# Key sums by TensorE for eight head pairs, denominators by one VectorE pass, silus of tile 0 in pairs, and a new planned order

## The chip, the cores and the metric

The kernel runs on one core of one Trainium2 chip. The metric is the device time of one execution in microseconds (us). The core has a matrix engine (TensorE, PE in the profile; PEld is its weight load), a vector engine (VectorE, DVE), a scalar engine (ScalarE, ACT), GpSimd (POOL) and a sync engine (SyncE, SP) that issues DMAs. Each engine runs its own instructions in the order in which the program gives them; engines wait for one another through semaphores.

## The reference

A linear attention with exponential features feeds a two-layer perceptron. There are 8 batches, 8 heads, 576 positions, head size 64, 128 features, and 4608 tokens of width 512 with an inner width of 2048.

```python
def phi(x):                       # x is q or k, scaled
    proj = einsum('bhsd,md->bhsm', x, omega)
    h = proj - sum(x * x, -1, keepdims=True) / 2
    return exp(h - max(h, -1, keepdims=True)) / sqrt(m)
kv  = einsum('bhsm,bhsd->bhmd', phi(k), v)
z   = sum(phi(k), axis=2)                         # the key sums
num = einsum('bhsm,bhmd->bhsd', phi(q), kv)
den = einsum('bhsm,bhm->bhs', phi(q), z)[..., None] + 1e-06
x   = (num / den), heads side by side             # 4608 x 512
h   = x @ w_in
out = (h * sigmoid(h)) @ w_out
```

## The kernel before

**Attention.** The work goes in 32 rounds n, each one pair of heads of one batch. A round has 9 chunks (NC) of 128 rows: four of the first head, one mixed chunk (MID) whose upper and lower 64 rows belong to different heads, four of the second. Per round and for k and q: `project` (L262) and `project_mid` (L269) on TensorE, row maxima `top` (L276, L278), row sums of squares `square_sum` (L254) and the exponent's shift `shift` (L282, L283) on VectorE, and the exponential on ScalarE, straight out of PSUM for n < 8 (DIRECT, `expo` L298), and after a VectorE pass (`lower`, L303 and L306) for the others. Then the key sums: `sums` adds the chunks on GpSimd with five instructions (L318, L320, L323), `zsum` multiplies with ones on TensorE (L327), so that the sum stands in every partition, and `zcopy` takes it to SBUF with four copies on ScalarE (L335, L336). The denominators: `products` makes e times z on VectorE with three instructions (L362), `denom` reduces them and takes the reciprocal (L369, L370). `normal` scales the query features on GpSimd (L375), `turn` transposes them (L381), `kv` (L343) and `numer` (L399) make the numerators, and `x_high` and `x_low` (L413, L418) split the result into two parts of x.

**Perceptron.** It goes in 9 tiles t of 512 tokens and 16 steps f per tile. Tile t < 8 takes positions 0 to 511 of batch t, so tile 0 needs rounds 0 to 3; tile 8 takes what is left over. `stage1` (L495) makes 12 matmuls into one bank of PSUM ring "h", which has two banks, `silu` (L500, L501) two activations, `g_low` (L505) one VectorE pass that frees the bank, and `stage2` (L513) 12 matmuls, two steps later (LAG). Each of the 32 weight blocks is prepared on the chip during tile 0: one pass on ScalarE (L442), three on VectorE (L456, L458, L462), two on GpSimd (L476, L480). The exponential and the silu lie in different activation tables of ScalarE, so a change between them costs a table load, which the trace puts on the line of the next activation.

**Order.** The program's order is made by a planner, `Plan.run`. Every piece of work is a unit with an engine, a duration, a key (its due time), units it comes after, and ring slots it takes and frees. The planner plays the engines forward with these durations and gives out, at each moment, the ready unit with the smallest key. The result is only an order of instructions on each engine; what waits for what on the chip is set by data and buffers. `at`, `clock`, START_MLP, PRO and STEP make the keys. The rounds n < 4 (LEAD) are given keys 11 us apart.

Of the kernel before, what the change touches and what calls it, by code (L numbers as in the profile page):

```python
# [56 lines left out]
CALM = 0.5  # L57


def clock(step):  # L60
    return START_MLP + SLOW * min(step, 16) + STEP * max(step - 16, 0)


class Plan:
# [6 lines left out]
    def add(self, name, eng, dur, key, fn, after=(), order=(), alloc=(), free=(), banks=0, table=None, lat=0.0):  # L71
# [9 lines left out]
    def run(self):  # L81
        end, first = {}, {}
        slots = {r: [] for r in RINGS}
# [27 lines left out]
        def bank_pools(u):  # L111
# [3 lines left out]
            if u["key"] < START_MLP - 1:  # L115
                pools.append("h")
# [14 lines left out]
        while any(ready.values()):  # L131
            best = None
            for e, us in ready.items():
                pick, least = None, None
                for u in us:
# [21 lines left out]
                    t = max(t, free_at[e])  # L157
# [30 lines left out]
            order.append(u)  # L188
            for c in children.get(n, ()):
# [8 lines left out]
def attention_mlp(ctx: ExitStack, tc: tile.TileContext, qT, kT, qn, kn, v, om_in, w_in, w_out, out):  # L198
# [19 lines left out]
    prod = const.tile([P, NC, M + 1], F32, tag="prod", name="prod")  # L218
    nc.gpsimd.memset(prod, GUARD)
# [328 lines left out]
    for n in range(NWIN):  # L548
        calm = n < LEAD
        for i, who in enumerate("kq"):  # L550
# [25 lines left out]
            for j in range(3):  # L576
                add(("top", n, who, j), "DVE", 0.3 if j == 2 else 0.7,
                    at(n, 3 * i + 1 + 0.1 * j, o + 1.2 + (4.5 if j == 2 else 0.1 * j)),
                    lambda n=n, who=who, j=j: top(n, who, j), after=[md if j == 2 else pj])
            if calm:  # L580
                add(("nb", n, who, 0), "DVE", 0.45, at(n, 3 * i + 1.5, 0), lambda n=n, who=who: shift(n, who, every),
                    after=[("top", n, who, j) for j in range(3)] + [("ssum",) + w], free=[("ss",) + w])
            else:
                add(("nb", n, who, 0), "DVE", 0.5, at(n, 0, o + 1.4), lambda n=n, who=who: shift(n, who, sides),
                    after=[("top", n, who, j) for j in range(2)] + [("ssum",) + w])
                add(("nb", n, who, 2), "DVE", 0.4, at(n, 0, o + 5.8), lambda n=n, who=who: shift(n, who, middle),
                    after=[("top", n, who, 2), ("ssum",) + w], free=[("ss",) + w])
# [15 lines left out]
        add(("v", n), "SP", 0.42, at(n, -8, 26 - 32), lambda n=n: load_v(n), order=[("v", n - 1)] if n else [],  # L603
            alloc=[("v", ("v", n))], lat=1.2)
# [16 lines left out]
        add(("ktt", n), "PE", 0.12, at(n, 6.7, 36.5), lambda ps, n=n: kv_turn(n, ps), after=[("kt", n)], banks=1,  # L621
# [3 lines left out]
        add(("prod", n), "DVE", 1.7, at(n, 8, 34.2), lambda n=n: products(n),  # L625
            after=e["q"] + [("zc", n)], order=[("den", n - 1)] if n else [], free=[("zb", n)])
        add(("den", n), "DVE", 1.6, at(n, 8.1, 34.4), lambda n=n: denom(n), after=[("prod", n)],
            alloc=[("den", ("den", n)), ("rd", ("rd", n))])
# [14 lines left out]
        dur = 1.4  # L643
        if follow:
# [3 lines left out]
            dur = 2.6  # L648
# [7 lines left out]
        add(("rest", n), "SP", 0.8, at(n, 20, 64), lambda n=n: keep_rest(n), after=[("xl", n, 0), ("xl", n, 1)], lat=0.2,  # L656
            free=[("x", t, k)])

    def weight(i, key, src, last, more=()):
        add(("wl",) + i, "SP", 0.42, key - 12, lambda: load_weight(src, i), order=[("wl",) + last] if last else [],  # L660
# [3 lines left out]
        for s in range(3):  # L664
            add(("wd",) + i + (s,), "DVE", (0.5, 0.78, 0.75)[s], key - 2 + 0.1 * s, lambda s=s: word(i, s),
# [3 lines left out]
                free=([("wraw",) + i] if s == 2 else [("wre",) + i] if s == 1 else []))  # L669
        add(("wh",) + i, "POOL", 0.9, key - 1, lambda: weight_high(i), after=[("wd",) + i + (2,)], alloc=list(more))  # L670
        add(("wlo",) + i, "POOL", 1.05, key, lambda: weight_low(i), after=[("wh",) + i], free=[("w32",) + i])

    last = None
    for f in range(NF):
# [6 lines left out]
        add(("keep", f), "SP", 0.42, clock(f + LAG) + 4, lambda f=f: keep_weight(f), after=[("wlo", "out", f)], lat=2.1,  # L681
# [3 lines left out]
    for k in range(NK):  # L685
        add(("restin", k), "SP", 0.8, clock(NF * B - 4), lambda k=k: load_rest(k),
            after=[("rest", n) for n in range(k, NWIN, NPAIR)], alloc=[(f"x{k}", ("x", B, k))], lat=2.2)
    done = None
    for i, (t, f) in enumerate(steps):
        key = clock(i)  # L690
        late = i >= total - LAG
        add(("get", t, f), "SP", 0.42, clock(i + LAG - AHEAD_OUT), lambda t=t, f=f: get_weight(t, f),
# [9 lines left out]
        add(("silu", t, f), "ACT", 1.22, key + STEP * 0.55, lambda t=t, f=f: silu(t, f), after=[("s1", t, f, NK - 1)],  # L702
# [3 lines left out]
        for j in range(4):  # L706
# [68 lines left out]
```

## Time and profile before

| | us |
|---|---|
| median of 3 runs | 1090.24 (1089.62 to 1092.56) |
| the profiled execution, its own time | 1089.61 |
| its span, first to last instruction | 1087.5 |
| PE busy | 1040.2 (96%) |
| DVE busy | 572.1 (53%) |
| ACT busy | 574.3 (53%) |
| POOL busy | 254.6 (23%) |

The busy times are averages over stages that differ. The page's forty slices show DVE at nine tenths up to about 190 us and at five tenths from there, PE at five to eight tenths at first and at nine from about 80 us on, and TensorE's granted clock below full speed up to about 100 us. So the span is read in stretches. A "chain" below is the chain of work that ended last, followed back from the last instruction.

### The profile page before, as it was taken

What the parts mean: (1) busy time and instruction counts of PE and PEld (TensorE: products, weight loads), DVE (VectorE), ACT (ScalarE), POOL (GpSimd) and SP (SyncE); (2) the same over time, 40 slices, a digit from 0 to 9 for tenths busy, and PEclk for the clock granted to TensorE, in tenths of its full rate; (3) what the DMA queues carried; (4) which work ended last, traced back from release to release, by engine and by line L of the source; (5) the groups of instructions that cost most, each with busy time, mean ns of one, the idle gap of its engine ahead of it and who ended that gap; (6) DMA issues with size and microseconds to landing.
All of it is one profiled execution on the core that took longest, in us unless ns stands there. A gap on an engine that the chain in (4) does not pass through costs nothing.

```text
span 1087.5 us, 16156 instructions
## 1 busy us (share of the span) xinstructions
PE 1040.2 (96%) x5900; PEld 825.2 (76%) x5900; DVE 572.1 (53%) x1109; ACT 574.3 (53%) x1077; POOL 254.6 (23%) x327
## 2 busy tenths in 40 slices
PE   5678998999999999999999999999999999999997
PEld 4456776677877778777877777777788778888886
DVE  6999988745555555545555555555555421111111
ACT  5677776565556555655556555655554543112111
POOL 3766655411222222121122211222222200000000
PEclk7868999999999999999999999999999999999999
DMA  7766777754435443544345444534442226333323
GB/s 274 248 220 228 271 249 243 238 176 141 141 123 176 128 126 118 175 141 130 123 133 172 126 136 141 180 122 137 130 157 89 65 83 213 97 97 126 107 97 97
DMA packets 66526, 167.84 MB, mean 154 GB/s; under 512 B 15632, under 2 KB 15760, under 8 KB 66448
## 3 DMA queue, kind: packets, MB, share of 16 engines
q1 hardware_dynamic: 65984, 166.23, 47.6%
q8 instruction: 47, 0.77, 0.3%
q10 hardware_dynamic: 464, 0.59, 0.2%
q14 instruction: 31, 0.25, 0.1%
HBM read 146.87 MB, written 19.92 MB: 153 GB/s over the span
## 4 chain that ended last, share of the span: by engine, by line
PE 80%; DVE 9%; ACT 6%; DMA 2%; issue 2%; POOL 0%; ACTq 0%; SPq 0%; DVEq 0%; POOLq 0%
PE ps_h L495 33%; PE ps_acc L513 32%; PE ps_att L262 5%; PE ps_att L343 3%; PE ps_att L381 2%; PE ps_att L399 2%; DVE w L458 1%; PE ps_att L327 1%; ACT L500 1%; DVE w L462 1%; PE ps_att L269 1%; DVE w L456 1%; DMA out<-ot 1%; DVE prod L362 1%; DMA wo_d<-wp 1%
## 5 line engine op out<-in xcount | busy, mean ns | idle before, releaser
L513 PE MATMUL ps_acc<-wo,gh 128*128 128x512 f32 x1152 | 369.0, 401 | 0.0
L500 ACT ACTIVATE gh<-ps_h 128x512 fp32r<-128x512 f32 x144 | 86.2, 599 | 308.4 <-PE ps_h L495 307.8
L505 DVE TENSOR_TENSOR gl<-ps_h,gh 128x512 fp32r<-128x512 f32 x144 | 97.9, 680 | 283.7 <-ACT ps_h L501 283.6
L513 PEld LDWEIGHTS ps_acc<-wo,gh 128*128 128x128 f32 x1152 | 206.2, 188 | 43.3
L495 PE MATMUL ps_h<-xh,wh 128*128 128x512 f32 x576 | 237.7, 413 | 0.3 <-ACT xh L413 0.3
L495 PE MATMUL ps_h<-xl,wh 128*128 128x512 f32 x576 | 225.5, 392 | 2.9 <-DVE xl L418 2.9
L495 PE MATMUL ps_h<-xh,wl 128*128 128x512 f32 x576 | 226.1, 393 | 0.0
L513 PE MATMUL ps_acc<-wo,gl 128*128 128x512 f32 x576 | 225.6, 392 | 0.0
L375 POOL TENSOR_TENSOR hq<-hq,rd 128x384 f32<-128x384 f32 x96 | 78.5, 846 | 380.0 <-DVE rd L370 375.3
L495 PEld LDWEIGHTS ps_h<-xh,wh 128*128 128x128 f32 x576 | 108.6, 189 | 24.8 <-ACT xh L413 0.5
L495 PEld LDWEIGHTS ps_h<-xl,wh 128*128 128x128 f32 x576 | 108.9, 189 | 24.1 <-DVE xl L418 3.3
L495 PEld LDWEIGHTS ps_h<-xh,wl 128*128 128x128 f32 x576 | 108.6, 188 | 24.5
L513 PEld LDWEIGHTS ps_acc<-wo,gl 128*128 128x128 f32 x576 | 108.1, 188 | 23.4
L318 POOL TENSOR_TENSOR t<-hk 128x256 f32<-128x256 f32 x64 | 48.8, 781 | 202.7 <-ACT hk L312 190.5
L312 ACT ACT_TABLE_LOAD x48 | 61.6, 1283 | 55.7 <-DVE hq L303 49.6
L501 ACT ACTIVATE ps_h<-ps_h 128x512 f32<-128x512 f32 x144 | 85.4, 593 | 0.0
L500 ACT ACT_TABLE_LOAD x56 | 71.8, 1283 | 22.7 <-PE ps_h L495 22.0
L278 DVE TENSOR_REDUCE mxq<-ps_att 128x4 f32<-128x512 f32 x57 | 36.9, 685 | 85.4 <-PE ps_att L262 85.4
L362 DVE TENSOR_TENSOR prod<-hq,zb 128x512 f32<-128x512 f32 (+1 forms) x96 | 53.0, 607 | 41.1 <-ACT zb L336 40.8
L250 ACT ACTIVATE nat<-nat 128x576 f32<-128x576 f32 x64 | 44.3, 700 | 23.4 <-DMA nat<-kn 18.6
L381 PE MATMUL ps_att<-ident,hq 128*128 128x128 f32 x261 | 41.0, 284 | 6.0 <-DVE hk L306 1.6
L278 DVE TENSOR_REDUCE mxk<-ps_att 128x4 f32<-128x512 f32 x55 | 35.5, 686 | 16.8 <-PE ps_att L262 16.8
(120 smaller groups left out, 1199.1 us busy)
## 6 DMA issues: line engine op xcount, KB each, us to landing
wo<-wo_d SPq DMA_DIRECT2D x144, 512.0 KB, 3.4
rawk<-kT SPq DMA_DIRECT2D x32, 352.0 KB, 3.0
rawq<-qT SPq DMA_DIRECT2D x32, 352.0 KB, 4.0
v<-v SPq DMA_DIRECT2D x32, 320.0 KB, 3.0
nat<-kn SPq DMA_DIRECT2D x32, 288.0 KB, 3.1
nat<-qn SPq DMA_DIRECT2D x32, 288.0 KB, 3.3
wraw<-w_in SPq DMA_DIRECT2D x16, 512.0 KB, 4.1
wraw<-w_out SPq DMA_DIRECT2D x16, 512.0 KB, 4.8
```

The lines of the kernel that those rows point to most:

```text
L262: nc.tensor.matmul(ps[:, i * M : (i + 1) * M], raw[r, o : o + P], oms[r], start=True, stop=True)
L278: nc.vector.tensor_reduce(m[:, 5 * j : 5 * j + 4], ps.rearrange("p (c m) -> p c m", m=M), AX.X, ALU.max)
L312: nc.scalar.activation(h, h, AF.Exp)
L318: nc.gpsimd.tensor_tensor(t[:, j], e[:, 5 * j : 5 * j + 2], e[:, 5 * j + 2 : 5 * j + 4], ALU.add)
L362: nc.vector.tensor_tensor(prod[:, c, :M], e[:, c], zb[:, j].unsqueeze(1).broadcast_to([P, hi - lo, M]), ALU.mult)
L375: nc.gpsimd.tensor_tensor(e[:, c], e[:, c], rd[:, c].unsqueeze(2).broadcast_to([P, 3, M]), ALU.mult)
L381: nc.tensor.transpose(ps[:, i * P : (i + 1) * P], T["h", n, "q"][:, 3 * g + i], ident)
L495: nc.tensor.matmul(ph, w[:, k, :], x, start=k == 0 and n == 0, stop=k == NK - 1 and n == 2)
L500: nc.scalar.activation(gh, ph, AF.Silu)
L501: nc.scalar.activation(ph, ph, AF.Silu)
L505: nc.vector.tensor_tensor(gl, T["ph", t, f], T["gh", t, f].bitcast(F32), ALU.subtract)
L513: nc.tensor.matmul(T["po", t][j], g[:, js], w, start=f == 0 and n == 0, stop=f == NF - 1 and n == 2)
```

## The change

For n < 8, `sums`, `zsum` and `zcopy` go. `zsum_direct` makes the key sums with ten matmuls straight from the nine chunks: the mixed chunk against one of two masks (`sides_of`), the others against ones. `denom_direct` multiplies chunk by chunk from PSUM and accumulates in the same instruction: ten instructions of 128 columns, two of them on 64 partitions. For n >= 8 `sums`, `zsum` and `zcopy` stay, and the denominators are nine such instructions from SBUF. In tile 0, the silu of an even step waits for the matmuls of the step after it. The planner gets other durations, a rule that units with `port` and units on POOL exclude one another, a rule that PE's units take 1.7 times as long after a pause, and shifts the keys of early units by random numbers of nine fixed seeds.

```diff
+SHIFTS = (1000, 1089, 1092, 1094, 1104, 1123, 1144, 1173, 1236,)
+def shift_keys(units):
+    early = [u for u in units if u["key"] < 235]
+    for seed in SHIFTS:
+        r = random.Random(seed)
+        part, wide = ((0.02, 6.0), (0.06, 3.0), (0.2, 1.5))[seed % 3]
+        for u, d in [(u, r.gauss(0, wide)) for u in early if r.random() < part]:
+            u["key"] += d
...
-            banks=banks, table=table, lat=lat,
+            banks=banks, table=table, lat=lat, port=port or eng == "POOL",
...
-                    t = max(t, free_at[e])
+                    t = max(t, free_at[e], port if u["port"] else 0.0)
...
+            if e == "PE":
+                if t - free_at[e] > 2.5:
+                    warm = t + 4.0
+                if t < warm:
+                    dur *= 1.7
             free_at[e] = t + dur
+            if u["port"]:
+                port = t + dur
...
-            if u["key"] < START_MLP - 1:
+            if u["key"] < START_MLP - 1 and ("s1", 0, 0, 0) not in end:
                 pools.append("h")
...
-    prod = const.tile([P, NC, M + 1], F32, tag="prod", name="prod")
-    nc.gpsimd.memset(prod, GUARD)
+    sides_of = const.tile([P, 2, P], F32, tag="sides", name="sides")
+    nc.gpsimd.memset(sides_of, 0.0)
+    for j in range(2):
+        nc.gpsimd.memset(sides_of[j * D : (j + 1) * D, j], 1.0)
+    prod = const.tile([P, NC, M], F32, tag="prod", name="prod")
...
+    def zsum_direct(n, ps):
+        e = T["h", n, "k"]
+        for j in range(2):
+            nc.tensor.matmul(ps[:, j * M : (j + 1) * M], sides_of[:, j], e[:, MID], start=True, stop=False)
+            for i in range(4):
+                nc.tensor.matmul(ps[:, j * M : (j + 1) * M], ones, e[:, 5 * j + i], start=False, stop=i == 3)
+        T["z", n] = ps
+
+    def denom_direct(n):
+        e, z = T["h", n, "q"], T.pop(("z", n))
+        den = new("den", [P, NC])
+        for c in range(NC):
+            for j in range(2) if c == MID else [int(c > MID)]:
+                r = slice(j * D, (j + 1) * D) if c == MID else slice(0, P)
+                nc.vector.tensor_tensor_reduce(
+                    out=prod[r, c], in0=e[r, c], in1=z[r, j * M : (j + 1) * M], scale=1.0, scalar=GUARD, op0=ALU.mult,
+                    op1=ALU.add, accum_out=den[r, c : c + 1],
+                )
+        T["rd", n] = rd = new("rd", [P, NC])
+        nc.vector.reciprocal(rd, den)
...
-    def products(n):
+    def denom(n):
         e, zb = T["h", n, "q"], T.pop(("zb", n))
-        for j, (lo, hi) in enumerate(((0, 4), (4, 5), (5, 9))):
-            c = slice(lo, hi)
-            nc.vector.tensor_tensor(
-                prod[:, c, :M], e[:, c], zb[:, j].unsqueeze(1).broadcast_to([P, hi - lo, M]), ALU.mult
+        den = new("den", [P, NC])
+        for c in range(NC):
+            j = (c >= MID) + (c > MID)
+            nc.vector.tensor_tensor_reduce(
+                out=prod[:, c], in0=e[:, c], in1=zb[:, j], scale=1.0, scalar=GUARD, op0=ALU.mult, op1=ALU.add,
+                accum_out=den[:, c : c + 1],
             )
-    def denom(n):
-        den = new("den", [P, NC])
-        nc.vector.tensor_reduce(den, prod, AX.X, ALU.add)
         nc.vector.reciprocal(rd, den)
...
+        if n < DIRECT:
+            add(zn, "PE", 2.3, at(n, 6.2, 31), lambda ps, n=n: zsum_direct(n, ps), after=e["k"], order=[("mid", n, "q")],
+                banks=1, free=[("h", n, "k")])
+        else:
+            add(("sums", n), "POOL", 3.3, at(n, 6, 25), lambda n=n: sums(n), after=e["k"], order=[("sums", n - 1)] if n > DIRECT else [],
...
+        if n < DIRECT:
+            add(("den", n), "DVE", 2.8, at(n, 8, 34.2), lambda n=n: denom_direct(n), after=e["q"] + [zn],
+                order=[("den", n - 1)] if n else [], alloc=[("den", ("den", n)), ("rd", ("rd", n))], free=[bk(zn)])
+        else:
+            add(("den", n), "DVE", 2.4, at(n, 8, 34.2), lambda n=n: denom(n), after=e["q"] + [("zc", n)], port=True,
...
-        add(("silu", t, f), "ACT", 1.22, key + STEP * 0.55, lambda t=t, f=f: silu(t, f), after=[("s1", t, f, NK - 1)],
+        pair = t == 0 and f % 2 == 0
+        add(("silu", t, f), "ACT", 1.12, key + STEP * (1.55 if pair else 0.55), lambda t=t, f=f: silu(t, f),
+            after=[("s1", t, f + pair, NK - 1)],
             alloc=[("gh", ("gh", t, f))], table="silu")
...
+    shift_keys(plan.units.values())
```

The units with `port` are the weight passes on VectorE, `shift`, and `denom` for n >= 8; the three products and the pass `denom_direct` are not among them.

## Rows read from the trace of the kernel before

**Rows 1.** Stretches: us, then busy us of PE, PEld, DVE, ACT, POOL; clock, DMA.

```profile
0.00:30.00 30.00, 18.86 (x144) 14.77 (x144) 21.36 (x39) 18.18 (x55) 11.97 (x20) 0.77 0.73 261
30.00:90.00 60.00, 38.48 (x268) 26.26 (x263) 58.72 (x98) 41.24 (x124) 39.88 (x45) 0.74 0.75 245
90.00:210.00 120.00, 111.65 (x638) 85.65 (x639) 110.52 (x177) 85.42 (x170) 75.20 (x78) 0.99 0.74 248
210.00:1000.00 790.00, 789.28 (x4499) 630.99 (x4498) 370.16 (x780) 411.52 (x695) 127.52 (x187) 1.00 0.43 134
```

**Rows 2.** The chain that ended last: start us, us, engine, tile, line, instructions.

```profile
16.68 0.43 PE ps_h L269 x2
...
38.76 0.21 DVE mxk L276
...
83.70 2.89 DVE prod L362 x3
86.59 0.73 DVE xl L418 x2
...
99.48 0.60 DVE gl L505
...
102.60 1.28 ACT L298
...
104.16 1.92 ACT hq L298 x7
...
107.95 0.60 ACT gh L500
...
127.28 0.26 PE ps_att L269 x2
...
140.85 0.67 PE ps_att L327 x2
...
207.07 2.73 PE ps_acc L513 x12
```

**Rows 3.** VectorE by line, 0 to 90 us: count, busy us, mean ns, idle before.

```profile
L362 DVE TENSOR_TENSOR prod<-hq,zb 128x512 f32<-128x512 f32 (+1 forms) x15 | 10.2, 735 | 0.2
L458 DVE SCALAR_TENSOR_TENSOR w<-wre,w 128x512 uint32<-128x512 uint32 x9 | 9.4, 1046 | 0.1
L462 DVE SCALAR_TENSOR_TENSOR w<-wraw,w 128x512 uint32<-128x512 uint32 x9 | 8.4, 936 | 0.3
L456 DVE TENSOR_SCALAR w<-wraw 128x512 uint32<-128x512 uint32 x10 | 7.6, 765 | 0.0
L369 DVE TENSOR_REDUCE den<-prod 128x9 f32<-128x1161 f32 x5 | 6.8, 1360 | 0.1
...
L283 DVE SCALAR_TENSOR_TENSOR nbk<-nbk,sqk 128x9 f32<-128x9 f32 (+2 forms) x8 | 4.7, 590 | 0.3
...
L282 DVE TENSOR_TENSOR nbk<-mxk,sqk 128x9 f32<-128x9 f32 (+2 forms) x8 | 3.1, 385 | 0.3
L282 DVE TENSOR_TENSOR nbq<-mxq,sqq 128x9 f32<-128x9 f32 (+2 forms) x6 | 2.4, 398 | 0.2
...
L283 DVE SCALAR_TENSOR_TENSOR nbq<-nbq,sqq 128x9 f32<-128x9 f32 (+2 forms) x6 | 1.5, 248 | 0.2
```

**Rows 4.** Same engine, whole span for two lines (ns min/median/max); 300 to 800 us for the third.

```profile
L456 DVE TENSOR_SCALAR w<-wraw x32: 410/422/1492, 13.1 to 202.2; 128x512 uint32<-128x512 uint32 x32
L458 DVE SCALAR_TENSOR_TENSOR w<-wre,w x32: 674/694/1771, 17.7 to 202.7; 128x512 uint32<-128x512 uint32 x32
...
L283 DVE SCALAR_TENSOR_TENSOR nbk<-nbk,sqk 128x8 f32<-128x8 f32 (+1 forms) x35 | 5.7, 164 | 1.2
```

**Rows 5.** GpSimd by line, 0 to 90 us: the three lines of the key sums.

```profile
L318 POOL TENSOR_TENSOR t<-hk 128x256 f32<-128x256 f32 x10 | 8.1, 816 | 12.2 <-ACT hk L298 12.2
L323 POOL TENSOR_TENSOR es<-es,hk 64x128 f32<-64x128 f32 x10 | 7.1, 708 | 2.7 <-ACT hk L298 2.1
L320 POOL TENSOR_TENSOR es<-t 128x256 f32<-128x256 f32 x5 | 4.1, 816 | 0.4
```

More of the change, by code (lines that the diff above doesn't have):

```diff
@@ L69, in __init__, with add @@
         self.freed_by = {}
-    def add(self, name, eng, dur, key, fn, after=(), order=(), alloc=(), free=(), banks=0, table=None, lat=0.0):
+    def add(self, name, eng, dur, key, fn, after=(), order=(), alloc=(), free=(), banks=0, table=None, lat=0.0, port=False):
         u = dict(
             name=name, eng=eng, dur=dur, key=key, fn=fn, after=list(after), order=list(order), alloc=list(alloc),
-            banks=banks, table=table, lat=lat,
+            banks=banks, table=table, lat=lat, port=port or eng == "POOL",
         )
@@ L79, in add, with run @@
             self.freed_by.setdefault(i, []).append(name)
-    def run(self):
+    def run(self, until=None):
         end, first = {}, {}
+        port, warm = 0.0, 0.0
         slots = {r: [] for r in RINGS}
@@ L580, in attention_mlp @@
             if calm:
-                add(("nb", n, who, 0), "DVE", 0.45, at(n, 3 * i + 1.5, 0), lambda n=n, who=who: shift(n, who, every),
-                    after=[("top", n, who, j) for j in range(3)] + [("ssum",) + w], free=[("ss",) + w])
-            else:
[L584 to L587, printed above, removed]
+                add(("nb", n, who, 0), "DVE", 0.36, at(n, 3 * i + 1.5, 0), lambda n=n, who=who: shift(n, who, every),
+                    after=[("top", n, who, j) for j in range(3)] + [("ssum",) + w], free=[("ss",) + w], port=True)
+            else:
+                add(("nb", n, who, 0), "DVE", 0.36, at(n, 0, o + 1.4), lambda n=n, who=who: shift(n, who, sides),
+                    after=[("top", n, who, j) for j in range(2)] + [("ssum",) + w], port=True)
+                add(("nb", n, who, 2), "DVE", 0.34, at(n, 0, o + 5.8), lambda n=n, who=who: shift(n, who, middle),
+                    after=[("top", n, who, 2), ("ssum",) + w], free=[("ss",) + w], port=True)
             for j in range(3):
@@ L616, in attention_mlp @@
         if not merged:
-            add(("kv", n), "PE", 1.5, at(n, 6.5, 28.5), lambda ps, n=n: kv(n, ps), after=e["k"] + [("v", n)], banks=1,
+            add(("kv", n), "PE", 1.2, at(n, 6.5, 28.5), lambda ps, n=n: kv(n, ps), after=e["k"] + [("v", n)], banks=1,
                 free=[("v", n), ("h", n, "k")])
@@ L620, in attention_mlp @@
             alloc=[("kt", ("kt", n))], free=[bk(kn_, 1 if merged else 0)])
[L621 removed]
+        add(("ktt", n), "PE", 0.2, at(n, 6.7, 36.5), lambda ps, n=n: kv_turn(n, ps), after=[("kt", n)], banks=1,
             free=[("kt", n)])
@@ L624, in attention_mlp @@
             alloc=[("kw", ("kw", n))], free=[bk(("ktt", n))])
[L625 to L628, printed above, removed]
+        if n < DIRECT:
[3 more added lines that the diff above has]
+            add(("den", n), "DVE", 2.4, at(n, 8, 34.2), lambda n=n: denom(n), after=e["q"] + [("zc", n)], port=True,
+                order=[("den", n - 1)] if n else [], alloc=[("den", ("den", n)), ("rd", ("rd", n))], free=[("zb", n)])
         plan.freed_by[("den", n)] = [("den", n)]
@@ L655, in attention_mlp @@
                 lambda n=n, i=i: x_low(n, i), after=[("xh", n, i)], free=[bk(nm, i)])
-        add(("rest", n), "SP", 0.8, at(n, 20, 64), lambda n=n: keep_rest(n), after=[("xl", n, 0), ("xl", n, 1)], lat=0.2,
+        add(("rest", n), "SP", 0.75, at(n, 20, 64), lambda n=n: keep_rest(n), after=[("xl", n, 0), ("xl", n, 1)], lat=0.2,
             free=[("x", t, k)])
     def weight(i, key, src, last, more=()):
-        add(("wl",) + i, "SP", 0.42, key - 12, lambda: load_weight(src, i), order=[("wl",) + last] if last else [],
+        add(("wl",) + i, "SP", 0.36, key - 12, lambda: load_weight(src, i), order=[("wl",) + last] if last else [],
             alloc=[("wraw", ("wraw",) + i)], lat=2.1)
@@ L664, in weight @@
         for s in range(3):
-            add(("wd",) + i + (s,), "DVE", (0.5, 0.78, 0.75)[s], key - 2 + 0.1 * s, lambda s=s: word(i, s),
+            add(("wd",) + i + (s,), "DVE", (0.43, 0.7, 0.7)[s], key - 2 + 0.1 * s, lambda s=s: word(i, s),
                 after=([("wd",) + i + (s - 1,), ("re",) + i] if s else [("wl",) + i]),
@@ L668, in weight @@
                 alloc=[] if s else [("w32", ("w32",) + i)],
-                free=([("wraw",) + i] if s == 2 else [("wre",) + i] if s == 1 else []))
-        add(("wh",) + i, "POOL", 0.9, key - 1, lambda: weight_high(i), after=[("wd",) + i + (2,)], alloc=list(more))
-        add(("wlo",) + i, "POOL", 1.05, key, lambda: weight_low(i), after=[("wh",) + i], free=[("w32",) + i])
+                free=([("wraw",) + i] if s == 2 else [("wre",) + i] if s == 1 else []), port=True)
+        add(("wh",) + i, "POOL", 0.64, key - 1, lambda: weight_high(i), after=[("wd",) + i + (2,)], alloc=list(more))
+        add(("wlo",) + i, "POOL", 1.29, key, lambda: weight_low(i), after=[("wh",) + i], free=[("w32",) + i])
     last = None
@@ L680, in attention_mlp @@
         last = ("out", f)
-        add(("keep", f), "SP", 0.42, clock(f + LAG) + 4, lambda f=f: keep_weight(f), after=[("wlo", "out", f)], lat=2.1,
+        add(("keep", f), "SP", 0.36, clock(f + LAG) + 4, lambda f=f: keep_weight(f), after=[("wlo", "out", f)], lat=2.1,
             free=[("wp", f)])
```

32 lines of the change are left out of this document (17 added, 15 removed).

## The prediction

> **What bounds the kernel now.** I read the stretches first [rows 1], because the page's busy shares mix two kernels: a start in which attention rounds 0 to 3 and the weight blocks are made, and a long steady part. From 210 to 1000 us PE is busy 789.3 of 790 us at full clock: nothing but PE work sets the time there, so an earlier or later start of that part arrives at the end undiminished. Between 30 and 90 us it is the other way round: DVE is busy 58.7 of 60 us, PE 38.5, at a mean clock of 0.74. From 90 to 210 both are nearly full, DVE 110.5 and PE 111.7 of 120, so PE has 8.3 us of idle time there and no more can be won from it. The second view, the chain, says the same with names: up to about 90 us it runs mostly over DVE. Round 3's last part of x, which tile 0 needs, is made at 86.59 us, straight behind another round's products of 2.89 us [rows 2]. So the change is worth what it takes out of DVE's queue before 90 us, less what it adds to PE after it.
>
> The third view, DVE by line up to 90 us [rows 3], shows that this queue is partly waiting. L458 takes 1046 ns on average and L456 765, while over the whole kernel their shortest are 674 and 410 and their medians 694 and 422 [rows 4]. The lines of the shift take 248 to 590 ns, and 164 in the middle of the kernel, where GpSimd is busy 16% of the time (127.5 of 790 us) and not 58% (51.9 of 90) [rows 1]. The excess up to 90 us: L456 7.6 - 10 x 0.42 = 3.4; L458 9.4 - 9 x 0.69 = 3.2; L462 8.4 - 9 x 0.69 = 2.2; L282 and L283 11.7 - 28 x 0.164 = 7.1. Together 15.9 us in which DVE counts as busy and waits [rows 3, 4]. The Trainium skill (SBUF — State Buffer, Who interferes with whom) gives a reason: a DVE instruction with two SBUF inputs and a GpSimd instruction that reads SBUF need the same port, and whichever comes second waits for the whole of the first. The rows agree in that the lines that stretch read two SBUF operands, or, L456, one in a fast form.
>
> **The change part by part.**
>
> *Denominators, n < 8.* Up to 90 us five rounds take 10.2 + 6.8 = 17.0 us, 3.4 each [rows 3]. In place come ten accumulating multiplications of 128 columns. No row shows that instruction. Its lower bound is the 0.21 us step of a 128-column reduction out of PSUM [rows 2], its upper bound the 3.4 us of now over nine chunks, 0.38 each, as if the new form saved nothing, with a small instruction of 0.164 behind it for the accumulator [rows 4]: 2.1 to 5.4 us a round. I take 0.26 each, nearer to the reduction, since that reads PSUM and hands out one number a row as this does: 2.6, a gain of 0.8 a round and 4.0 for five (6.5 gained to 10 lost). The reciprocal stays. The Trainium skill (VectorE: DVE Perf Modes, Two Vector instructions with no wait between them) says that an instruction which also writes out its accumulator is two. No row shows it; as a mechanism with a price from rows it is a rival below.
>
> *Key sums leave GpSimd.* Up to 90 us they are 8.1 + 7.1 + 4.1 = 19.3 us [rows 5] of 51.9 [rows 1], 37%. If the 15.9 us of waiting fall in proportion, DVE gains 5.9. The bounds are 0 (the weights' GpSimd passes move into the freed place and collide as often) and 12 (the new order also keeps the rest apart). I take the proportion: the planner now excludes overlap of `port` units and POOL, but that makes an order and no wait, and on the chip every engine runs on when its data is there.
>
> *The new order.* The 2.89 us of products ahead of round 3's x is an order that a plan with truer durations can mend. I take 2.0 of it (0 to 2.9).
>
> *Key sums come to PE.* Ten matmuls of 128 columns at L269's 0.26 us (full clock) or 0.43 (slow) [rows 2]: 2.6 or 4.3 a round, against 0.67 for L327 at full clock: +1.9, taken as +1.7, since back-to-back matmuls on the same ones overlap more than two after a change of shape. Rounds 0 to 4 fall in the 90 us in which PE idles 32.7 us [rows 1]: nothing, and if that cover is gone at most 3.6 a round. The chain there doesn't lengthen, as GpSimd's sums and ScalarE's four copies leave it. Rounds 5 to 7 lie in the full stretch: 3 x 1.7 = +5.1 (4 to 6).
>
> *ScalarE.* The copies and some table loads of 1.28 us [rows 2] go; ACT is busy 85 of 120 us [rows 1], so this only shortens waits. With less waiting on the port after 90 us too, I take 3 of PE's 8.3 idle us as gained (0 to 7).
>
> *Silus in twos* add a wait: the first silu of a pair waits for one more step of stage 1, and stage 1's next step waits, because ring "h" has two banks, for silu and `g_low` of that first step. Behind the waiting silu in ACT's queue stand copies and exponentials of the rounds. Costed at nothing: two steps of stage 2, 2 x 2.73 = 5.5 us [rows 2], are there to cover it. The price without that cover is a rival.
>
> *n >= 8.* DVE's denominators change form, at 370 busy us of 790 [rows 1]; PE has 0.7 us idle there: nothing. The memsets at the start run while the first loads come in: nothing.
>
> **Sum.** 4.0 + 5.9 + 2.0 = 11.9 us earlier at the start; +5.1 - 3 after it: -9.8 us. From the profiled execution's 1089.6 (span 1087.5 and 2.1 around it) that is 1079.8; the median of the runs lies 0.6 above it, so 1080.4, taken as 1080.
>
> **The rivals.**
>
> *The port really clears.* The new order keeps DVE's two-operand passes and GpSimd apart, so that 12 of the 15.9 us go before 90, and the shorter rounds save some more of PE's idle time, 4 us. 9.8 + 6.1 + 4 = 20: **1070**. For it: the keys of the kernel before put rounds 0 to 3 11 us apart, while the last of them is done at 86.59 us [rows 2], so its plan was far from the chip and a truer one has much to mend. Against: nothing on the chip holds the plan's times.
>
> *The accumulator is a second instruction.* Ten times 0.21 + 0.164 = 3.7 us a round, so the denominators lose 0.3 x 5 = 1.5 where I gain 4.0: 5.5 later, **1086**.
>
> *The change doesn't do what it says.* GpSimd's place is taken by its weight passes, the overlap stays and no order helps: 4.0 gained before 90, 5.1 lost after it: **1091**.
>
> *Slower: the two banks.* After a pair's second stage 1, ACT loads the table (1.28), runs two activations (2 x 0.60) and DVE makes gl (0.60): 3.1 us with empty queues [rows 2]. If a set of eight exponentials (1.92 for seven of them, so 2.2) stands ahead on ACT and a round's denominators (2.6) on DVE it is 7.9, against 5.5 of cover: PE waits 2.4 us, eight times in tile 0: 19 us on 1080, **1099**. It decides from 2.4 us of queue ahead of silu and gl together; then PE idles again between 90 and 210. For it: both engines are over 70% busy there. Against: the planner knows the ring.
>
> **How the numbers follow.** My forecast, 1074 to 1086, has a chance of 0.45; the cleared port 0.18; the accumulator 0.08; no effect 0.13; the two banks 0.16. A measurement of this kernel tells about 0.3% from no change, 3.3 us, so faster means under 1087.0. Faster: 0.45 + 0.18 + 0.06 of the accumulator's 0.08 = 0.69. Same: the 0.02 left, and 0.13 = 0.15. Slower: 0.16. The range 1067 to 1094 leaves out the far end of the cleared port (0.06) and most of the two banks (0.13). It takes in the bounds of the single terms: the dearest accumulating pass, 10 us lost in place of 4.0 gained, alone gives 1094.
>
> **What would show it.** Right: PE becomes full 8 to 14 us earlier than at 90 us; L456 under 0.65 us on average up to there; the new pass at 0.21 to 0.31 us a step; PE as full as before from then on. Wrong: an accumulating pass over 0.35 us; DVE's weight passes still near 0.9 us; idle time of PE ahead of L495 in tile 0, released by DVE's L505, which would be the two banks; or key sums on PE well over 2.6 us each in the full stretch.

## The result and the profile after

The changed kernel takes 1078.54 us (median of 4, 1077.01 to 1079.87), beside runs of the kernel before of 1090.94 on the same chip: a ratio of 0.9885, 95% interval 0.9863 to 0.9908. Run again beside other runs of the kernel before it came to 0.9903 (0.9881 to 0.9924). The forecast was 1080. The profiled execution took 1077.01 us, its span is 1075.2, 12.3 under that of before.

The stretches of the changed kernel (us from the start, length, then busy us of PE, PEld, DVE, ACT and POOL, granted clock, DMA share, GB/s), to be held against [rows 1]:

```profile
30.00:90.00 60.00, 49.76 (x402) 39.89 (x399) 55.00 (x178) 45.67 (x129) 29.39 (x30) 0.91 0.85 285
90.00:210.00 120.00, 115.86 (x698) 92.92 (x697) 95.45 (x228) 72.06 (x142) 57.56 (x57) 0.99 0.70 239
210.00:1000.00 790.00, 789.19 (x4483) 630.41 (x4482) 349.26 (x1094) 411.23 (x693) 125.80 (x184) 1.00 0.43 134
```

Between 30 and 90 us PE works 11 us more than before, at a granted clock of 0.91 and not 0.74, and GpSimd 10.5 us less. From 90 to 210 PE idles 4.1 us, where it was 8.3. From 210 us on nothing has changed for PE.

The start of the full stretch can be read to the tenth from VectorE's and PE's instructions: round 3's last `x_low` ends at 73.2 us, where [rows 2] have 86.59 for its beginning, with its second part ending at 87.3. So the start came 14.1 us earlier, and 1.8 of that was lost again behind it (the span fell by 12.3).

As the start moved, stretches with fixed ends compare different work. Cut at its own start, each kernel has two stretches; first the kernel before, below it the changed one:

```profile
0.00:87.30 87.30, 56.04 (x404) 40.45 (x404) 77.48 (x132) 58.34 (x176) 50.83 (x62) 0.76 0.75 251
87.30:1087.50 1000.20, 984.18 (x5497) 784.76 (x5497) 494.66 (x979) 515.92 (x901) 203.74 (x265) 1.00 0.46 146
```

```profile
0.00:73.20 73.20, 59.43 (x493) 48.37 (x493) 62.42 (x212) 51.50 (x154) 31.28 (x40) 0.88 0.83 280
73.20:1075.20 1002.00, 988.35 (x5551) 791.82 (x5551) 468.68 (x1362) 510.15 (x887) 192.21 (x250) 1.00 0.46 147
```

Up to the start VectorE is busy 15.1 us less (77.5 and 62.4) and idle 1.0 more (9.8 and 10.8): that is the 14.1. Behind it PE is busy 4.2 us more, by 54 more matmul records, and idle 2.4 us less (16.0 and 13.6): that is the 1.8.

VectorE's lines up to 90 us (count, busy us, mean ns, idle before), against [rows 3]; L500, L502 and L506 are the weight passes, L307 and L308 the shift, L369 the new denominators:

```profile
L502 DVE SCALAR_TENSOR_TENSOR w<-wre,w 128x512 uint32<-128x512 uint32 x13 | 9.6, 738 | 1.9 <-ACT wre L486 1.5
L506 DVE SCALAR_TENSOR_TENSOR w<-wraw,w 128x512 uint32<-128x512 uint32 x12 | 9.3, 786 | 0.3
L500 DVE TENSOR_SCALAR w<-wraw 128x512 uint32<-128x512 uint32 x14 | 8.9, 646 | 0.0
...
L369 DVE CUSTOM_DVE_ANT_0 prod<-hq,ps_att 128x128 f32<-128x128 f32 (+1 forms) x20 | 4.6, 282 | 0.1
...
L369 DVE DVE_READ_ACCUMULATOR2_ANT den<- 128x1 f32 (+1 forms) x50 | 4.0, 81 | 0.0
...
L307 DVE TENSOR_TENSOR nbk<-mxk,sqk 128x9 f32<-128x9 f32 (+2 forms) x8 | 2.6, 325 | 0.2
L308 DVE SCALAR_TENSOR_TENSOR nbk<-nbk,sqk 128x9 f32<-128x9 f32 (+2 forms) x8 | 1.9, 240 | 0.3
...
L307 DVE TENSOR_TENSOR nbq<-mxq,sqq 128x9 f32<-128x9 f32 (+2 forms) x8 | 1.4, 174 | 0.2
...
L308 DVE SCALAR_TENSOR_TENSOR nbq<-nbq,sqq 128x9 f32<-128x9 f32 (+2 forms) x7 | 1.2, 169 | 0.2
```

By the prediction's own reckoning the waiting in them is 9.6 - 13 x 0.69 = 0.6, 9.3 - 12 x 0.69 = 1.0, 8.9 - 14 x 0.42 = 3.0 and 7.1 - 31 x 0.164 = 2.0: 6.6 us, where it was 15.9. At the same time 12 to 14 weight passes of each kind are done by 90 us, and not 9 or 10. Reckoned in the same way up to each kernel's own start, where both have done 18 of the two longer passes, 9 or 10 of the short one and 26 instructions of the shift, the waiting is 1.2 + 2.0 + 1.4 = 4.6 us (longer passes, short pass, shift), where it was 5.4 + 3.4 + 5.9 = 14.7.

The new denominators in VectorE's order of time (start us, us, engine, line, instruction):

```profile
16.90 0.28 DVE L369 CUSTOM_DVE_ANT_0 prod<-hq,ps_att 128x128 f32<-128x128 f32 x1
17.10 0.08 DVE L369 DVE_READ_ACCUMULATOR2_ANT den<- 128x1 f32 x1
17.10 0.28 DVE L369 CUSTOM_DVE_ANT_0 prod<-hq,ps_att 128x128 f32<-128x128 f32 x1
17.31 0.09 DVE L369 DVE_READ_ACCUMULATOR2_ANT den<- 128x1 f32 x1
...
19.30 0.22 DVE L374 RECIPROCAL rd<-den 128x9 f32<-128x9 f32 x1
```

The accumulator is read out by an instruction of its own, 81 ns, but the next multiplication starts with it. The step is 0.21 us, 0.30 behind the two on 64 partitions, and ten of them take 2.4 us (16.90 to 19.30).

PE's waits in tile 0 of the changed kernel (in brackets the idle time before and what ended it):

```profile
73.25 0.50 PE L539 MATMUL ps_h<-xl,wh 128*128 128x512 f32 x1 [1.50 <-DVE xl L462]
...
82.69 0.80 PE L539 MATMUL ps_h<-xh,wh 128*128 128x512 f32 x1 [3.87 <-DVE gl L549]
...
129.69 0.47 PE L539 MATMUL ps_h<-xh,wh 128*128 128x512 f32 x1 [1.00 <-DVE gl L549]
...
161.17 0.77 PE L539 MATMUL ps_h<-xh,wh 128*128 128x512 f32 x1 [2.70 <-DVE gl L549]
```

Three waits for `g_low`, 7.6 us together: stage 1 stands still because both banks of ring "h" are still held. In the kernel before, none of PE's waits was of this kind. ScalarE and VectorE ahead of the first of them:

```profile
78.07 0.60 ACT L544 ACTIVATE gh<-ps_h 128x512 fp32r<-128x512 f32 x1
78.56 0.59 ACT L545 ACTIVATE ps_h<-ps_h 128x512 f32<-128x512 f32 x1
```

```profile
78.45 0.98 DVE L506 SCALAR_TENSOR_TENSOR w<-wraw,w 128x512 uint32<-128x512 uint32 x1
79.35 1.48 DVE L500 TENSOR_SCALAR w<-wraw 128x512 uint32<-128x512 uint32 x1
80.76 1.28 DVE L303 TENSOR_REDUCE mxq<-ps_att 128x4 f32<-128x512 f32 x2
81.95 1.27 DVE L549 TENSOR_TENSOR gl<-ps_h,gh 128x512 fp32r<-128x512 f32 x2
```

The first silu is done at 79.15 us, but `g_low` starts at 81.95: VectorE first has a weight pass of 1.48 us, 1.06 of it waiting, and two maxima. GpSimd's pass at that time is the following one; it ends at 80.55, and the weight pass at 80.83:

```profile
78.96 1.59 POOL L524 TENSOR_TENSOR wl<-w,wh 128x512 fp32r<-128x512 f32 x1
```

### The profile page after: what moved, and what is told of

It reads as the page before. It is cut to its first block, busy times and chain, and to the rows that moved or that the text cites. A ratio compares the mean times of both kernels' runs of the same rounds, so it can differ in the third digit from the quotient of the medians.

```text
span 1075.2 us, 16814 instructions
## 1 busy us (share of the span) xinstructions
PE 1047.8 (97%) x6044; PEld 840.2 (78%) x6044; DVE 531.1 (49%) x1573; ACT 561.7 (52%) x1041; POOL 223.5 (21%) x289
## 4 chain that ended last, share of the span: by engine, by line
PE 88%; DVE 4%; DMA 3%; ACT 2%; issue 1%; POOL 1%; SPq 0%; ACTq 0%; DVEq 0%; POOLq 0%
PE ps_h L539 36%; PE ps_acc L557 36%; PE ps_att L287 5%; PE ps_att L389 3%; PE ps_att L443 3%; PE ps_att L425 2%; PE ps_att L294 1%; PE ps_att L352 1%; DMA rawk<-kT 1%; DMA wo_d<-wp 1%; DVE w L502 1%; DVE prod L369 1%; DVE w L500 1%; DMA wraw<-w_in 1%; DVE mxq L303 0%
## 5 line engine op out<-in xcount | busy, mean ns | idle before, releaser
L544 ACT ACTIVATE gh<-ps_h 128x512 fp32r<-128x512 f32 x144 | 86.1, 598 | 298.6 <-PE ps_h L539 298.0
L343 POOL TENSOR_TENSOR t<-hk 128x256 f32<-128x256 f32 x48 | 34.8, 746 | 211.3 <-ACT hk L337 211.3
L409 DVE CUSTOM_DVE_ANT_0 prod<-hq,zb 128x128 f32<-128x128 f32 x216 | 47.9, 288 | 42.7 <-ACT zb L382 41.1
L275 ACT ACTIVATE nat<-nat 128x576 f32<-128x576 f32 x64 | 44.2, 700 | 15.9 <-DMA nat<-kn 10.9
L429 ACT COPY en<-ps_att 128x384 f32<-128x384 f32 x84 | 38.3, 479 | 7.9 <-PE ps_att L425 6.3
```

Source lines behind the costliest of these rows:

```text
L275: nc.scalar.activation(nat, nat, AF.Square, scale=SCALE * 0.5**0.5)
L409: nc.vector.tensor_tensor_reduce(out=prod[:, c], in0=e[:, c], in1=zb[:, j], scale=1.0, scalar=GUARD, op0=ALU.mult, op1=ALU.add, accum_out= ...
L429: nc.scalar.copy(T["en", n][:, 3 * g * P : 3 * (g + 1) * P], T.pop(("t", n, g))[:, : 3 * P])
L544: nc.scalar.activation(gh, ph, AF.Silu)
```

## Experiments

The first theory was the prediction's: the start is VectorE's queue, and less work and less waiting on the port shorten it (A). Against it: the new plan is the gain (B). The table has the runs, each against the kernel before on its own chip. The last three columns are of one profiled execution: "start" is the end of round 3's last `x_low`; "waiting" is VectorE's up to there, by the prediction's reckoning (0.42, 0.69 and 0.164 us for an instruction of the three kinds); "idle" is PE's idle time from the start to the end of the span. Executions of one order (the changed kernel, `after_again`, `late_den_old`, whose orders agree up to the start) differ by 2 us in "start" and 1.3 in "idle".

| run | us | ratio (95%) | start | waiting | idle |
|---|---|---|---|---|---|
| before | 1090.94 | | 87.3 | 14.7 | 16.0 |
| after | 1078.54 | 0.9885 (0.9863 to 0.9908) | 73.2 | 4.6 | 13.6 |
| after_again | 1078.14 | 0.9903 (0.9881 to 0.9924) | 73.0 | 4.6 | 13.0 |
| work_only | 1081.97 | 0.9947 (0.9929 to 0.9964) | 76.9 | 6.5 | 13.8 |
| order_only | 1097.85 | 1.0091 (1.0070 to 1.0112) | 87.6 | 9.9 | 21.8 |
| no_seeds | 1087.83 | 0.9991 (0.9979 to 1.0003) | 75.3 | 5.9 | 17.4 |
| other_seeds | 1086.64 | 0.9977 (0.9965 to 0.9988) | 75.6 | 6.5 | 15.7 |
| no_pair | 1079.68 | 0.9921 (0.9905 to 0.9938) | 74.1 | 4.6 | 12.9 |
| sums_back | 1085.22 | 0.9962 (0.9947 to 0.9978) | 78.4 | 8.9 | 15.4 |
| z_twice | 1086.87 | 0.9981 (0.9967 to 0.9996) | 80.9 | 4.6 | 11.6 |
| den_four | 1082.82 | 0.9948 (0.9929 to 0.9966) | 78.5 | 4.6 | 13.2 |
| late_den_old | 1078.54 | 0.9901 (0.9879 to 0.9923) | 75.0 | 4.6 | 12.3 |
| search_pair | 1080.73 | 0.9921 (0.9898 to 0.9943) | 73.2 | 6.5 | 13.7 |
| search_single | 1081.61 | 0.9941 (0.9920 to 0.9963) | 81.2 | 7.3 | 9.5 |

**The work alone.** The planner's rules, durations, keys and silus are those of before. The edit, cut, against the changed kernel:

```diff
-SHIFTS = (1000, 1089, 1092, 1094, 1104, 1123, 1144, 1173, 1236,)
+SHIFTS = ()
-                    t = max(t, free_at[e], port if u["port"] else 0.0)
+                    t = max(t, free_at[e])
-                if t < warm:
+                if False:
-        pair = t == 0 and f % 2 == 0
+        pair = False
...
```

> The new key sums and denominators alone, with the planner, the durations, the keys and the single silus of the kernel before. Theory A (less work and less waiting on VectorE in the first 90 us is the gain): 4.0 + 5.9 us earlier, 5.1 more on PE, 3 less idle there: 8 us under the kernel before, 1083, with PE full about 10 us earlier than at 87 us. Theory B (the plan with truer costs is the gain): no gain from the work and 5 us more on PE, 1091 to 1096.

It takes 0.9947 of the kernel before, 5.8 us under it, and its start comes 10.4 us earlier. Round 3's last `x_low` in it:

```profile
76.14 0.63 DVE L462 TENSOR_TENSOR xl<-ps_acc,xh 128x512 fp32r<-128x512 f32 x1
76.68 0.21 DVE L462 TENSOR_TENSOR xl<-ps_att,xh 128x64 fp32r<-128x64 f32 x1
```

Theory A holds for about half of the gain. That the forecast's terms for denominators and port (9.9 us) meet the 10.4 is in part chance: up to the start VectorE is busy 14.0 us less than before and idle 3.6 more, and 3.1 of that is one wait for a round's key sums on PE.

```profile
0.00:76.90 76.90, 60.16 (x494) 47.95 (x494) 63.52 (x211) 52.24 (x155) 28.70 (x38) 0.89 0.78 266
```

Behind its start PE idles 13.8 us, as in the changed kernel (13.6) and not as before (16.0).

**The order alone.** The new rules without the seeds, with the old key sums, products and reduction in the place of the new units; the products are `port` units here.

```diff
...
+        add(("sums", n), "POOL", 3.3, at(n, 6, 25), lambda n=n: sums(n), after=e["k"],
+        add(("prod", n), "DVE", 1.7, at(n, 8, 34.2), lambda n=n: products(n), port=True,
+        add(("den", n), "DVE", 1.6, at(n, 8.1, 34.4), lambda n=n: denom(n), after=[("prod", n)],
...
```

> The new planner (port rule, slow PE after a pause, durations, silus in pairs), without the seeds, for the old work: key sums on GpSimd, four copies, three products and a reduction. Theory A: 2 to 4 us under the kernel before, 1087 to 1089, with VectorE's weight passes still near 0.9 us up to 90 us. Theory B: most of the gain, 1080 to 1083.

Neither theory's number: it is slower than before, by 0.9%, 9.9 us. Rounds 2 and 3 end almost together, at 84.6 and 87.6 us:

```profile
83.75 0.81 DVE L465 TENSOR_TENSOR xl<-ps_acc,xh 128x512 fp32r<-128x512 f32 x2
86.82 0.82 DVE L465 TENSOR_TENSOR xl<-ps_acc,xh 128x512 fp32r<-128x512 f32 x2 [0.53 <-ACT xh L460]
```

VectorE's waiting up to the start is less than before, 9.9 us and not 14.7, but its idle time there is 15.6 and not 9.8 us (71.99 busy of 87.60), and behind the start PE idles 21.8 us:

```profile
0.00:87.60 87.60, 58.66 (x404) 43.27 (x404) 71.99 (x132) 56.44 (x175) 49.59 (x65) 0.77 0.73 246
```

So a planner that knows the port doesn't by itself make a better order: what it takes off the waiting comes back as idle time.

**The seeds.**

```diff
-SHIFTS = (1000, 1089, 1092, 1094, 1104, 1123, 1144, 1173, 1236,)
+SHIFTS = ()
```

> The changed kernel without the random shifts of the keys. Theory A: within 4 us of the changed kernel, 1078 to 1083, as work and port set the time. Theory B: the shifts found by searching are a large part of the gain, 1085 or more.

Theory A's bound of 1083 is missed: without the seeds the changed kernel is level with the one before (0.9991), though its start is only 2 us later than with them. Theory B's 1085 or more is met. Most of the loss lies behind the start: PE idles 17.4 us there, and 13.6 with the seeds, and is busy 2.8 us longer.

```profile
75.30:1083.90 1008.60, 991.19 (x5572) 792.19 (x5570) 470.89 (x1389) 519.04 (x900) 196.86 (x253) 1.00 0.44 147
```

```diff
-SHIFTS = (1000, 1089, 1092, 1094, 1104, 1123, 1144, 1173, 1236,)
+SHIFTS = (2000, 2089, 2092, 2094, 2104, 2123, 2144, 2173, 2236,)
```

> The changed kernel with nine other seeds, not searched for (each old one plus 1000). If the nine seeds matter because they were selected: at or above the kernel without seeds, 1087 to 1100. If any stirring of the keys is good: about 1080.

Nine seeds that nobody selected give 0.9977 and 1086.64 us, near the kernel without any. So what the nine seeds bring, 8 to 10 us, is selection and not stirring, as far as one other set can show it.

**Silus by themselves.**

```diff
-        pair = t == 0 and f % 2 == 0
+        pair = False
```

> The changed kernel with every silu of tile 0 due by itself, seeds kept (the order is planned anew from the same keys). Two banks: PE waits 7.6 us for g_low in the first 230 us of the changed kernel, so without pairs most of it is won, 1072 to 1075, unless the table loads (1.28 us each) come back into the chain. Rival (the loads that pairs save are worth more): 1081 or more, with more table loads in tile 0.

Neither number is met: 0.9921 against 0.9885 and 0.9903, between the two expectations, and the intervals touch. The waits for `g_low` ahead of stage 1 are gone, but one of 3.7 us ahead of `turn` (L425) is new, and there are more table loads. ScalarE from 73 to 210 us with single silus, and below it with pairs (table loads; L544 silu, L323 and L337 exponentials):

```profile
L544 ACT ACT_TABLE_LOAD x12 | 15.4, 1283 | 0.2
L323 ACT ACT_TABLE_LOAD x9 | 11.5, 1283 | 6.5 <-DVE nbk L308 4.6 <-DVE nbq L308 1.7
L337 ACT ACT_TABLE_LOAD x2 | 2.6, 1283 | 0.0
```

```profile
L544 ACT ACT_TABLE_LOAD x8 | 10.3, 1283 | 0.6 <-PE ps_h L539 0.5
L323 ACT ACT_TABLE_LOAD x5 | 6.4, 1283 | 2.2 <-DVE nbq L308 1.9 <-DVE nbk L308 0.3
L337 ACT ACT_TABLE_LOAD x2 | 2.6, 1283 | 0.0
```

With pairs eight loads, 10.3 us of ScalarE, are saved for 7.6 us of PE's waiting. The sum is 0 to 4 us in favour of the pairs, and the nine seeds were selected for an order with pairs.

The next four edits leave the order of the changed kernel as it is and change one cost in it. The ground for them:

> The changed kernel once more, beside the runs of the kernel before that the next three share. Expected as measured: 0.9885 of the kernel before, 12 us under it. It is the ground against which the next three are read.

It came out as expected, 0.9903.

**GpSimd's key sums put back.** Five instructions a round for n < 8, their result unused.

```diff
-            add(zn, "PE", 2.3, at(n, 6.2, 31), lambda ps, n=n: zsum_direct(n, ps), after=e["k"], order=[("mid", n, "q")],
+            add(zn, "PE", 2.3, at(n, 6.2, 31), lambda ps, n=n: (sums(n), zsum_direct(n, ps)), after=e["k"], order=[("mid", n, "q")],
```

> The changed kernel in its own order, with the five GpSimd instructions of the old key sums put back for n < 8; their result is not used. Theory (GpSimd's sums held the shared port, and VectorE and the weight passes waited): 5 to 10 us over the changed kernel, VectorE's two-operand passes up to 90 us longer by 6 us or more in sum, PE full later than at 73 us. Rival (GpSimd was off the path, the gain came from VectorE's fewer and shorter instructions and the new order): within 2 us of the changed kernel.

0.9962 against 0.9903, 6.4 us on 1090, and 7.1 by the medians: the theory's range. The start is 5.4 us later. VectorE's passes up to 90 us, and its time up to the start:

```profile
L502 DVE SCALAR_TENSOR_TENSOR w<-wre,w 128x512 uint32<-128x512 uint32 x12 | 9.8, 817 | 0.4
L506 DVE SCALAR_TENSOR_TENSOR w<-wraw,w 128x512 uint32<-128x512 uint32 x11 | 9.6, 880 | 0.3
L500 DVE TENSOR_SCALAR w<-wraw 128x512 uint32<-128x512 uint32 x13 | 9.1, 714 | 1.7 <-POOL wl L524 1.7
```

```profile
0.00:78.40 78.40, 62.20 (x493) 50.46 (x493) 66.81 (x212) 51.43 (x154) 47.57 (x65) 0.89 0.80 267
```

With the shift's lines (8.7 us for 30) the passes hold 1.5 + 2.0 + 3.6 + 3.8 = 10.9 us of waiting, against 6.8 reckoned in the same way in `after_again`: 4.1 more, less than the 6 expected. Up to the start it is 8.9 against 4.6, and VectorE is busy 4.5 us longer (66.8 and 62.3). The other 0.9 of the 5.4 is idle time, in which VectorE waits 1.7 us for GpSimd's `wl` ahead of a weight pass (L500): GpSimd's own longer queue. What GpSimd holds longer by reading hk was not separated.

**Key sums on PE made twice.** The same ten matmuls into the same bank, once more; the result is the same.

```diff
+        for j in range(2):
+            nc.tensor.matmul(ps[:, j * M : (j + 1) * M], sides_of[:, j], e[:, MID], start=True, stop=False)
+            for i in range(4):
+                nc.tensor.matmul(ps[:, j * M : (j + 1) * M], ones, e[:, 5 * j + i], start=False, stop=i == 3)
```

> The changed kernel in its own order, with the ten matmuls of the new key sums made twice for n < 8. Theory (free in the start stage, where PE idles, paid in full where PE is the bound, rounds 5 to 7): 2.2 to 2.4 us a round, 7 us over the changed kernel, up to 9 with the clock. Rival 1 (the key sums lie on the chain of every round): 18 us or more over it. Rival 2 (PE has room in tile 0 too): under 2 us.

The number was met, 0.9981 against 0.9903, 8.5 us, and the reason was not: the second set is not free in the start. Up to the start VectorE is as busy with the key sums once (`after_again`) as, below it, twice, but idle 10.7 and 18.2 us, which is 7.5 of the 7.9 us by which the start comes later:

```profile
0.00:73.00 73.00, 60.17 (x493) 49.45 (x493) 62.31 (x212) 51.44 (x154) 31.30 (x40) 0.86 0.82 280
73.00:1075.60 1002.60, 989.60 (x5551) 792.77 (x5551) 468.61 (x1362) 510.73 (x887) 192.41 (x250) 0.99 0.45 147
```

```profile
0.00:80.90 80.90, 68.23 (x593) 57.79 (x593) 62.66 (x212) 51.33 (x154) 31.62 (x40) 0.92 0.76 261
80.90:1086.50 1005.60, 994.05 (x5611) 798.19 (x5611) 468.32 (x1363) 510.76 (x887) 192.15 (x250) 1.00 0.45 146
```

The key sums of five rounds, 0 to 4, lie ahead of the start, as round 4's denominators stand before round 3's `x_low`. At four of the five VectorE waits for the second set (in brackets), 5.8 us together:

```profile
18.68 0.29 DVE L373 CUSTOM_DVE_ANT_0 prod<-hq,ps_att 128x128 f32<-128x128 f32 x1 [1.42 <-PE ps_att L364]
33.55 0.29 DVE L373 CUSTOM_DVE_ANT_0 prod<-hq,ps_h 128x128 f32<-128x128 f32 x1 [1.25 <-PE ps_h L364]
49.33 0.29 DVE L373 CUSTOM_DVE_ANT_0 prod<-hq,ps_h 128x128 f32<-128x128 f32 x1 [1.40 <-PE ps_h L364]
77.62 0.29 DVE L373 CUSTOM_DVE_ANT_0 prod<-hq,ps_att 128x128 f32<-128x128 f32 x1 [1.74 <-PE ps_att L364]
```

A set takes 2.2 us at full clock. With one set, in the changed kernel and in `after_again`, VectorE waits for none of the five. So one set has room there, and a second one overruns it by 1.3 to 1.7 us a round: rival 1 holds in the start, but for the second set only, and the run gives no price for the first. Of the 11 us by which this execution's span is longer, 1086.5 against 1075.6, only 3.0 came behind the start, where three rounds add 6.6 us of matmuls. PE's busy time grew by 4.4 there and its idle time fell by 1.4; the other 2.2 of the 6.6 are open.

**Denominators in the old form, out of PSUM.** Four products and one reduction for n < 8.

```diff
...
+        nc.vector.tensor_tensor(prod[:, :4, :M], e[:, :4], zj[0], ALU.mult)
+        for j in range(2):
+            r = slice(j * D, (j + 1) * D)
+            nc.vector.tensor_tensor(prod[r, MID, :M], e[r, MID], z[r, j * M : (j + 1) * M], ALU.mult)
+        nc.vector.tensor_tensor(prod[:, 5:, :M], e[:, 5:], zj[1], ALU.mult)
+        nc.vector.tensor_reduce(den, prod, AX.X, ALU.add)
...
```

> The changed kernel in its own order, with the denominators of n < 8 in the old form out of PSUM: four products and one reduction in place of ten accumulating instructions. By the rows 3.4 us and not 2.4 a round. Theory (VectorE's queue is the bound of the start, so its shorter denominators are worth their time): 0.8 to 1.0 us for each of the five rounds of the start, 4 to 5 us over the changed kernel. Rival (after the change PE and the round's chain bind the start and VectorE no longer does): under 2 us.

0.9948 against 0.9903, 4.9 us, as the theory has it, and the start 5.5 later: VectorE is busy 4.5 us longer up to it. Its reduction alone takes what more than six of the new instructions take:

```profile
L373 DVE TENSOR_REDUCE den<-prod 128x9 f32<-128x1161 f32 x5 | 6.8, 1365 | 0.2
```

**Denominators of the 24 later rounds in the old form.**

```diff
...
+            nc.vector.tensor_tensor(
+                prod[:, c, :M], e[:, c], zb[:, j].unsqueeze(1).broadcast_to([P, hi - lo, M]), ALU.mult
+            )
...
+        nc.vector.tensor_reduce(den, prod, AX.X, ALU.add)
...
```

> The changed kernel in its own order, with the old products and reduction for the 24 rounds n >= 8. Theory: PE is full from 210 us on, so this is worth nothing: within 1.5 us of the changed kernel. Rival: the shorter denominators shorten waits of PE behind VectorE: 3 us or more over it.

0.9901 against 0.9903: nothing, as expected, though VectorE is 17.8 us busier from 210 to 1000 us (367.1 against 349.3) and PE as full as before:

```profile
210.00:1000.00 790.00, 789.14 (x4484) 630.14 (x4483) 367.09 (x774) 412.57 (x696) 125.83 (x184) 1.00 0.41 135
```

**A longer search.** More seeds, each kept if the planner's own clock put the start of tile 2 earlier; once with pairs and the nine seeds, once with single silus and from none.

```diff
-SHIFTS = (1000, 1089, 1092, 1094, 1104, 1123, 1144, 1173, 1236,)
+SHIFTS = (1000, 1089, 1092, 1094, 1104, 1123, 1144, 1173, 1236, 30058, 30093, 30120, ...)
```

> The changed kernel with 17 more seeds, picked one after the other where the planner's own start of tile 2 came earlier: 314.65 in place of 318.0 in its clock. If the planner ranks orders as the chip does: 3 us under the changed kernel, 1075. If its ranking holds only for large differences (8 to 20 us, as between the orders tried so far): anything from 1074 to 1084.

> The changed kernel with single silus and 21 seeds searched for from nothing in the same way, start of tile 2 at 314.1 in the planner's clock. If the planner ranks as the chip does: 4 us under the changed kernel, 1074, and pairs aren't needed. If not: 1076 to 1086.

Neither beats the changed kernel: 0.9921 and 0.9941. The planner's clock for the start of tile 2, and what the chip made of the order:

```
order          planner   ratio on the chip
order_only      342.6    1.0091
other_seeds     332.8    0.9977
no_seeds        327.4    0.9991
no_pair         325.9    0.9921
before          322.5    1
work_only       322.2    0.9947
after           318.0    0.9885, 0.9903
search_pair     314.7    0.9921
search_single   314.1    0.9941
```

It tells the worst order from the best, but not `work_only` from `before`, nor the last three apart, and it puts `no_pair` far too late. The rules of `before` and `work_only` don't know the port, so their clock leaves the waiting on it out.

## Why the prediction was right, and where it was not

**What bounds the kernel** was read rightly: the gain is made before tile 0 is full, and arrives at the end. The start moved by 14.1 us (forecast 11.9) and 1.8 was given back behind it (forecast 5.1 - 3 = 2.1). That it is VectorE's queue shows in VectorE's own time: 15.1 us less busy up to the start, 1.0 more idle.

**Denominators**, forecast 0.8 us a round and 4.0 in all: 2.4 us a round, so 1.0 gained and 5 in all, and 4.9 by `den_four`. The step I chose, 0.26 us, was a little long: eight of ten are at the lower bound, 0.21. The Trainium skill's rule (VectorE: DVE Perf Modes, Two Vector instructions with no wait between them) is borne out in that the accumulator is a second instruction, 81 ns in the trace. The rival made of it was priced wrongly, as if the second instruction came after the first's end: it runs under the next multiplication.

**Key sums off GpSimd**, forecast 5.9: mis-sized. The waiting fell from 15.9 to 6.6 us by 90 us, and from 14.7 to 4.6 up to each start: 10.1, nearer to the 12 of the cleared port than to the proportion's 5.9. With the old rules it is already 6.5 (`work_only`), so 8.2 came with the work and 1.9 with the new order. `sums_back` shows that 4.3 are GpSimd's key sums (6.4 us of time with GpSimd's own queue). The other 3.9 of the 8.2 are open: the old products, which read two SBUF operands too, went at the same time. The Trainium skill (SBUF — State Buffer, Who interferes with whom) says that the loser waits for the whole instruction. The trace agrees where it was read: the weight pass at 79 us, 1.06 us over its 0.42, ends 0.28 us behind GpSimd's. That the planner keeps the port's users apart did not show as a gain of its own: `order_only` is slower.

**Key sums on PE**: rounds 0 to 4 at nothing agrees with the trace as far as VectorE's waits go, as it waits for none of these five sets in the changed kernel. But the reason given, that PE idled 32.7 us there, doesn't carry it: PE still idles 12.8 us of 73 up to the start (`after_again`), and `z_twice` pays 7.9 us for a second set. In `work_only`, with another order, VectorE waits 3.1 us for a single set. What PE's own queue paid for the first sets is not measured. Rounds 5 to 7, forecast 5.1: PE's busy time behind the start grew by 4.2.

**The order**: the 2.0 us at the start did not come as described. Another round's denominators still stand straight ahead of round 3's x, from 69.91 to 72.52 us, and VectorE idles no less than before. I counted the rest as luck. From `work_only` to the changed kernel it is 0.9947 to 0.9885 or 0.9903, 5 to 7 us, and this is a sum of two large terms: the new rules with pairs lose 4.8 us (`no_seeds` against `work_only`), the nine seeds win 9.6 to 11.6 (0.9991 to 0.9903 or 0.9885). I also took keys 11 us apart, against 86.59 on the chip, as a sign that the plan was far from the chip. Keys only rank units.

**PE behind the start**: 3 idle us forecast, 2.4 won; without the seeds nothing was (17.4 idle, 16.0 before).

**Silus in twos**: costed at nothing, and the rival was eight waits of 2.4 us. Its mechanism, named as a sign of being wrong, is in the trace three times, 7.6 us together, at the place it named: 2.8 us of VectorE's queue ahead of `g_low` at 79 us, over its 2.4, though it is a weight pass and two maxima and not a round's denominators. It didn't decide: PE didn't wait at five of the eight pairs, and the pairs save eight table loads. That they are worth anything is not shown: 0 to 4 us.

**Rounds n >= 8**: nothing forecast, nothing found (`late_den_old`).

So 1080 against 1078.54 rests on a bound that was read rightly and on terms that came out near (denominators, the matmuls of rounds 5 to 7, PE's idle time). The port was sized 4.2 too small and the order's 2.0 did not come, and these two partly cancel, which is luck. It is luck too that the shipped order has the selected seeds, for which the sum has no term: the same work and rules without them give 0.9991. What stays open is what PE's queue paid for the first key sums, and 3.9 us of the port's shorter waits.

## What to carry to other kernels

Where an in-order engine sets a start stage, count the waiting inside its busy time. A line whose mean is far over its shortest can have a rival for a port; here the rival's work put back cost 6.4 us, more than the 4.9 of the engine's own shorter work. Don't cost a moved instruction at nothing because its new engine has idle time over a stretch; ask how much room the engine that needs its result leaves it, in each round. Here one set of matmuls found room and a second one did not. Compare stretches from each kernel's own start, since fixed ends hold different work once the start moves. An order found by search belongs to the work it was searched for, so compare a change with and without it: here the work alone won 5.8 us, the new rules alone lost 9.9, and nine selected seeds won 9.6 to 11.6.

## What the runs showed of the hardware that was not expected

The multiplication that also accumulates takes 0.28 us for 128 columns, whether its second operand lies in PSUM (282 ns) or both lie in SBUF (288 ns on the page of the changed kernel), and steps at 0.21 us in a row although an 81 ns read of the accumulator follows each. Three rounds' second sets of key sums, 6.6 us of matmuls behind the start, raised PE's busy time there by 4.4 us and lengthened that stretch by 3.0 (one execution each, and starts of one order differ by 2).
